# Opening stage of an agent-attention and squared-ReLU kernel: the first batch in 32-column tiles, tables made in place, weight parts decoded in another order

## The chip, the cores and the metric

The kernel runs on one core of a Trainium2 chip. The metric is the device time of one execution in microseconds (us); of several runs the median counts.

Five engines work side by side, each in the order of its own instructions: TensorE (PE, matmuls; its weight loads are listed as PEld), VectorE (DVE), ScalarE (ACT), GpSimd (POOL) and SyncE (SP, which issues the transfers). They wait for each other by semaphores.

## The reference

Four batches of 12,480 queries, keys and values with 128 channels go through an attention by way of 49 agents; each token then goes through a feed-forward layer with 2,048 hidden units.

```python
def sm(a, b):
    s = scale * (a @ b.transpose(0, 2, 1))
    s = s - s.max(-1, keepdims=True)
    e = np.exp(s)
    return e / (e.sum(-1, keepdims=True) + 1e-09)
a2k = sm(agents, k)
agent_v = a2k @ v
q2a = sm(q, agents)
x = (q2a @ agent_v).reshape(B * S, D)     # 49920 x 128
h = np.maximum(x @ w_in, 0.0)             # 128 x 2048
return (h * h @ w_out).astype(np.float32) # 2048 x 128
```

Both weights arrive as 64-bit numbers, which the kernel must turn into 32-bit ones itself.

## The kernel before, in words

**The main loop.** `agent_v @ w_in` is computed once for each batch: a table of 49 rows and 2,048 columns. The hidden layer of a token is then its 49 softmax weights times this table. The table is kept as a rounded part and a remainder (`aw_hi`, `aw_ex`), so that two products on TensorE give nearly 32-bit accuracy: `first(k)` issues for two steps of k together 4 matmuls with `aw_hi` and 4 small ones with `aw_ex`. `hidden(k)` makes r = ReLU (ACT), r times h (DVE; for odd k in place in PSUM), the rounded square `g_hi` (ACT) and its remainder `g_lo` (DVE for odd k, POOL for even k). `second(k)` multiplies these by the second weight, which is also kept as a rounded part and a remainder (`wo_hi`, `wo_lo`), 6 matmuls for each k, LAG = 4 steps later. There are 832 steps of k, 16 for each group of 960 queries (8 for each half), taken in 416 pairs. The queries' softmax of the next group (`queries`) and the attention of the next batch (`background`: `scores`, `maxima`, `values`, `whole_sums`, `tables`) are laid between them in small steps, spread over 0.88 of a batch.

**The opening.** Nothing of the main loop can run before the table of batch 0 exists. While the flag `alone` is set, every instruction goes through `queued`, so each engine's order is the order of the code. The stages are:

- `WARM` dummy matmuls, then the scores of 13 blocks of keys (12 of 8 x 128 keys, one of 192): in each, one matmul of 128 keys against the agents of two batches at once (98 columns, of which 49 are used). DVE keeps a running maximum (`mx`), ACT copies the scores out of PSUM. Between blocks 3 and 10, six of the eight parts of `w_in` are decoded.
- `decoded`: one ACT instruction (absolute value) and five DVE instructions for each part of 256 columns. A part of `w_in` ends in one POOL addition (`make_w_in`), a part of `w_out` in one ACT cast and two POOL operations (`make_w_out`).
- `maxima`: over all keys, through a transpose and two small matmuls; the result is `mb`.
- `whole_exps` (DVE subtraction, ACT exponential), `whole_values` (one matmul for each 128 keys, with the exponentials of two such groups side by side, 98 columns), and `add_weights` (POOL adds up the exponentials for the sums). The other ten weight parts are decoded in between; the last two of `w_out` come after the tables.
- `whole_sums` and `tables`: the four chunks of the table, ACT rounding each into `aw_hi`, DVE writing the remainder into `aw_lo`, and five transfers for each chunk that carry the remainder to other partitions (rows 98 to 127 of `aw_hi`, and four places of `aw_ex`).

Keys and values share a ring of 11 buffers (`ahead`), the raw weight parts a ring of 8 (`raw`), PSUM three double banks (`ps_h`, tiles `h`), one bank for the background (`ps_a`, tiles `psa`) and one for the output (`ps_o`). Line 59 (`queued`) is the line that the profile shows for all that is issued in written order.

Of the kernel before, what the change touches and what calls it, by code (L numbers as in the profile page):

```python
# [29 lines left out]
WARM = 16  # L30
PRE = 11
RAW = 8
# [5 lines left out]
def agent_attention_relu2(ctx: ExitStack, tc: tile.TileContext, qT, kT, v, agT, w_in, w_out, outT):  # L38
# [12 lines left out]
    NQ = P // 32  # L51
    scale = 1.0 / math.sqrt(C)
# [29 lines left out]
    qp = ctx.enter_context(tc.tile_pool(name="qp", bufs=2))  # L82
    ps_h = ctx.enter_context(tc.tile_pool(name="ps_h", bufs=3, space=PSUM))
# [6 lines left out]
    nc.gpsimd.memset(ones, 1.0)  # L90
    ident = const.tile([P, P], F32, name="ident")
# [8 lines left out]
    def asked_for(dec, src):  # L100
        raw = dec.tile([P, WCH, 2], U32, name="raw", bufs=RAW)
# [4 lines left out]
    def ask_w_in(dec, n):  # L106
        return asked_for(dec, w_in.bitcast(U32)[:, 2 * n * WCH : 2 * (n + 1) * WCH])

    def ask_w_out(dec, n):
        c = slice(n * WCH // C, (n + 1) * WCH // C)  # L110
        return asked_for(dec, w_out.bitcast(U32).rearrange("(c p) d -> p c d", p=P)[:, c, :])

    def decoded(dec, raw):
        low, high = raw[:, :, 0], raw[:, :, 1]

        t = dec.tile([P, WCH], U32, name="t")
        act.activation(t.bitcast(F32), high.bitcast(F32), AF.Abs)
# [14 lines left out]
    def make_w_in(dec, n, raw):  # L132
        t, rest = decoded(dec, raw)
        pool.tensor_add(win[:, n * WCH : (n + 1) * WCH], t, rest)

    def make_w_out(dec, n, raw):
        c = slice(n * WCH // C, (n + 1) * WCH // C)
        t, rest = decoded(dec, raw)
# [3 lines left out]
        pool.tensor_add(lo, t, rest)  # L142

# [29 lines left out]
    def scores(b, i, kt):  # L173
        st = state.setdefault(b, {"s": []})
        _, rows, nt = blocks[i]
        if alone[0]:
            h = ps_h.tile([P, 2, 512], F32, name="h")[:rows, :, :].rearrange("p h (t x) -> p h t x", x=P)
            n = nt // 2
            for t in range(nt):
                out = h[:, t // n, t % n, : 2 * NA]  # L180
                keys = kt[:, t * rows : (t + 1) * rows]
                pe.matmul(out, keys, ag[:, :2, :].rearrange("c b a -> c (b a)"), start=True, stop=True)
            sv = h[:, :, :n, :NA]
        else:
            sv = bank()[:rows, : nt * NA].rearrange("p (t a) -> p t a", a=NA)
            for t in range(nt):
                tiled(sv[:, t, :], kt[:, t * rows : (t + 1) * rows], ag[:, b, :])
# [6 lines left out]
        if alone[0]:  # L194
            s, mx = (x.rearrange("p (h t) a -> p h t a", h=2) for x in (s, mx))
# [44 lines left out]
    def whole_values(b, i, vt):  # L240
        st = state[b]
        _, rows, nt = blocks[i]
        e = st["s"][i][:rows, :nt, :]
        if i == 0:
            st["pv"] = ps_h.tile([P, 2, 512], F32, name="h")
        for t in range(nt):
            pair = e[:, t - t % 2 : t - t % 2 + 2, :].rearrange("p t a -> p (t a)")
            pe.matmul(
                st["pv"][:C, t % 2, : 2 * NA], vt[:rows, t, :], pair,
                start=(i == 0 and t < 2), stop=(i == NK - 1 and t >= nt - 2),  # L250
            )

    def add_weights(b, i):
        st = state[b]
        _, rows, nt = blocks[i]
        if i > 0:
            es = st["mx"][:rows, :nt, :]
            pool.tensor_add(es, es if i > 1 else st["s"][0], st["s"][i][:rows, :nt, :])

    def whole_sums(b):  # L260
        st = state[b]
        e1 = small.tile([P, 2, NA], F32, name="e1")
        dve.reduce_sum(e1[:, 0, :], st["mx"].rearrange("p t a -> p a t"), axis=AX.X)
        dve.tensor_copy(e1[:, 1, :], e1[:, 0, :])
        yield
        av = st["avT"] = small.tile([C, K2], F32, name="avT")
        if "pv" in st:
            act.copy(av[:, :NA], st["pv"][:C, 0, :NA])
            dve.tensor_add(av[:, :NA], av[:, :NA], st["pv"][:C, 1, NA : 2 * NA])
        else:  # L270
            dve.tensor_copy(av[:, :NA], st["av"])
        dve.tensor_copy(av[:, NA:], av[:, :NA])
        pz = bank()
        pe.matmul(pz[:K2, :1], e1.rearrange("p h a -> p (h a)"), ones[:, :1], start=True, stop=True)
        rl = st["rl"] = small.tile([K2, 1], F32, name="rl")
        dve.tensor_scalar_add(rl, pz[:K2, :1], 1e-9)
        dve.reciprocal(rl, rl)
# [21 lines left out]
    def tables(b):  # L299
# [3 lines left out]
        ex = st["lo"] = aw.tile([P, NCH // NQ, P], F32R, name="aw_ex")  # L303
        for n in range(FF // 512):
            yield
            cs = slice(n * 512, (n + 1) * 512)
            pw = bank()
            pe.matmul(pw[:K2, :], av, win[:, cs], start=True, stop=True)
# [7 lines left out]
            yield  # L316
# [7 lines left out]
    def queries(g):  # L324
# [10 lines left out]
        dve.reduce_max(m, sv, axis=AX.X)  # L335
        e = qp.tile([TP, NT, NA], F32, name="e", bufs=1)
# [97 lines left out]
    def background(b):  # L434
# [15 lines left out]
        yield from whole_sums(b)  # L450
        yield from tables(b)

    STEPS = NK * 2 + 5 + NK * 4 + 1 + 3 * (FF // 512)
# [13 lines left out]
    NW = FF // WCH  # L467
# [5 lines left out]
    with tc.tile_pool(name="pre", bufs=PRE) as pre, tc.tile_pool(name="dec", bufs=2) as dec:  # L473
        def warm(n):
            idle = bank()
            for _ in range(n):
                pe.matmul(idle[:, :P], ones, ones, start=True, stop=True)

        raws = {}
        kts, vts = [], []  # L480

        def next_values():
            vts.append(load_values(0, len(vts), pre, "ahead"))

        between = {i: n for n, i in enumerate((3, 4, 6, 7, 9, 10))}
        for i in range(NK):
            kts.append(load_keys(0, i, pre, "ahead"))
            if 1 <= i <= NW:
                raws[i - 1] = ask_w_in(dec, i - 1)
            if i == NK - 3:  # L490
                q0 = queries(0)
                next(q0)
            run(scores(0, i, kts[i]))
            if i in between:
                make_w_in(dec, between[i], raws.pop(between[i]))
        next_values()
        for n in range(6):
            next_values()
            raws[NW + n] = ask_w_out(dec, n)
# [5 lines left out]
        next(top)  # L505
        warm(2)
# [3 lines left out]
        for i in range(2):  # L510
            add_weights(0, i)
        between = {i: n for n, i in enumerate((0, 1, 3, 4, 6, 7, 9, 10))}
        for i in range(NK):
            if i + 3 < NK:
                whole_exps(0, i + 3, dve)
            if i + 2 < NK:
                add_weights(0, i + 2)
            if i == NK - 1:
                ends = whole_sums(0)
                next(ends)  # L520
            whole_values(0, i, vts[i])
            next(q0, None)
            if i in between:
                n = between[i]
                if n < 2:
                    make_w_in(dec, NW - 2 + n, raws.pop(NW - 2 + n))
                    next_values()
                    raws[2 * NW - 2 + n] = ask_w_out(dec, NW - 2 + n)
                else:
                    make_w_out(dec, n - 2, raws.pop(NW + n - 2))  # L530
            if i >= 2 and len(vts) < NK:
                next_values()
        run(q0)
        run(ends)
        ahead = queries(1)
        next(ahead)
        run(tables(0))
        next(ahead)
        next(ahead)
        for n in range(NW - 2, NW):  # L540
            make_w_out(dec, n, raws.pop(NW + n))
    behind = [chain[eng] for eng in (nc.sync, nc.scalar, nc.vector, nc.gpsimd)]

    alone[0] = False
    ffn = ctx.enter_context(tc.tile_pool(name="ffn", bufs=4))
    todo = iter(())
    for k in range(total + LAG):
        if k < total:
            g, c = divmod(k, SLOTS)
            b, i = divmod(g, NB)  # L550
            if i == 0 and c == 0 and b + 1 < B:
                todo = background(b + 1)
                done = 0
            goal = (i * SLOTS + c + 1) * STEPS / (SPREAD * NB * SLOTS)
# [5 lines left out]
            if c >= 2 or g == 0:  # L560
# [46 lines left out]
```

## Time and profile before

| | |
|---|---|
| median of 3 runs | 2005.19 us (2005.07 to 2005.92) |
| the profiled execution: its time, its span | 2006.08 us, 2004.3 us |
| PE, PEld, DVE, ACT, POOL busy in the span | 98%, 74%, 84%, 86%, 59% |
| transfers: share of the 16 DMA engines | 19.9% |
| first `r` of the main loop (ACT) | at 96.97 us |

The busy shares are means over the whole span. In the 40 slices of the profile (50 us each) the first slice and a part of the second and third are the opening; from there on the slices are alike.

### The profile page before, as it was taken

The page shows a single profiled execution, that of the slowest core. Times are in us where ns is not written, and L with a number is a line of the kernel's source. Part 1 is how long each engine was busy: PE and PEld are TensorE (multiplying, and loading weights), DVE is VectorE, ACT ScalarE, POOL GpSimd, SP SyncE. Part 2 cuts the span into 40 slices and gives each one's busy share as a digit, 9 for nine tenths or more (in the row PEclk, how much of TensorE's full clock was granted, in tenths as well). Part 3 has the DMA queues.
Part 4 walks back from the last instruction along what each step waited for, and adds up shares of the span by engine and source line. Part 5 has one row for each costly group of instructions (what it writes and reads, how often), then busy time and mean ns, then how long its engine had stood idle before and what let it go on. Part 6 is the DMA issues. An engine that isn't in the chain of part 4 may idle for free. (4 is left out here: it accounts for less than half of the span.)

```text
span 2004.3 us, 44157 instructions
## 1 busy us (share of the span) xinstructions
PE 1966.5 (98%) x17240; PEld 1486.0 (74%) x17240; DVE 1677.2 (84%) x1852; ACT 1729.8 (86%) x2019; POOL 1191.0 (59%) x1054
## 2 busy tenths in 40 slices
PE   8699999999999999999999999999999999999999
PEld 7477777777777777777777777777777777777777
DVE  5678878888888888888888888888888888898887
ACT  2388888889988888889988898898999999999997
POOL 1545676655555666656555576665565656565555
PEclk8799999999999999999999999999999999999999
DMA  8242222111122221211122211211111111111100
GB/s 313 72 137 75 88 73 77 59 61 47 50 89 83 70 77 59 66 66 50 49 67 89 67 56 59 86 56 38 54 38 43 38 46 37 37 47 38 33 24 20
DMA packets 55991, 132.14 MB, mean 66 GB/s; under 512 B 6712, under 2 KB 35336, under 8 KB 55784
## 3 DMA queue, kind: packets, MB, share of 16 engines
q1 hardware_dynamic: 55784, 129.33, 19.9%
q8 instruction: 136, 2.23, 0.5%
q14 instruction: 71, 0.58, 0.1%
HBM read 80.97 MB, written 25.56 MB: 53 GB/s over the span
## 5 line engine op out<-in xcount | busy, mean ns | idle before, releaser
L405 POOL TENSOR_TENSOR g_lo<-gg,g_hi 128x480 fp32r<-128x480 f32 x832 | 999.9, 1223 | 706.1 <-DVE gg L59 458.8
L59 ACT ACTIVATE r<-h 128x960 f32<-128x960 f32 x832 | 801.8, 964 | 127.2 <-PE h L59 117.3
L59 ACT ACTIVATE g_hi<-r 128x960 fp32r<-128x960 f32 x832 | 837.6, 1007 | 35.5 <-issue 0.4
L59 DVE TENSOR_TENSOR h<-r,h 128x960 f32<-128x960 f32 x416 | 482.0, 1159 | 158.7 <-ACT r L59 153.5
L59 PE MATMUL o<-g_hi,wo_hi 128*128 128x480 f32 x1664 | 542.7, 407 | 0.6 <-DVE z L344 0.6
L59 DVE TENSOR_TENSOR gg<-r,h 128x960 f32<-128x960 f32 x416 | 477.6, 1148 | 44.2 <-ACT r L59 41.1
L59 DVE TENSOR_TENSOR g_lo<-h,g_hi 128x960 fp32r<-128x960 f32 x416 | 480.7, 1155 | 36.2 <-ACT g_hi L59 2.2
L59 PE MATMUL o<-g_hi,wo_lo 128*128 128x480 f32 x1664 | 499.3, 381 | 0.0
L59 PE MATMUL o<-g_lo,wo_hi 128*128 128x480 f32 x1664 | 497.8, 380 | 0.0
L59 PE MATMUL h<-w,aw_hi 128*128 128x480 f32 x1664 | 475.4, 397 | 14.4 <-DVE gg L59 12.3
L59 PEld LDWEIGHTS o<-g_hi,wo_hi 128*128 128x128 f32 x1664 | 280.8, 188 | 119.9 <-issue 65.2
L59 PEld LDWEIGHTS o<-g_lo,wo_hi 128*128 128x128 f32 x1664 | 312.6, 188 | 51.3
L59 PEld LDWEIGHTS o<-g_hi,wo_lo 128*128 128x128 f32 x1664 | 312.7, 188 | 51.1
L59 PEld LDWEIGHTS h<-w,aw_hi 128*128 128x128 f32 x1664 | 292.1, 189 | 73.2 <-DVE gg L59 21.0
L59 PE MATMUL h<-x,aw_ex 19*128 19x480 f32 x1664 | 204.0, 480 | 0.0
L59 PEld LDWEIGHTS h<-x,aw_ex 19*128 19x128 f32 x1664 | 80.0, 182 | 139.5 <-issue 139.2
L59 DVE COPY ob<-o 128x480 f32<-128x480 f32 x104 | 68.2, 656 | 41.5 <-PE o L59 41.4
L354 PEld LDWEIGHTS psa<-identr,pp 120*98 120x98 f32 x408 | 51.7, 165 | 8.9
L359 ACT CAST w<-psa 98x480 fp32r<-98x480 f32 x102 | 55.5, 544 | 2.4 <-PE h L59 0.5
L226 POOL TENSOR_TENSOR pp<-e,pp 120x392 fp32r<-120x392 f32 x51 | 49.3, 967 | 11.4 <-ACT pp L224 11.4
L345 POOL TENSOR_TENSOR e<-e,z 120x392 f32<-120x392 f32 x51 | 43.1, 845 | 16.1 <-ACT d L286 8.6
L171 PEld LDWEIGHTS psa<-ag,qt 128*32 128x32 f32 (+1 forms) x3200 | 37.9, 108 | 16.8 <-issue 15.8
(110 smaller groups left out, 845.9 us busy)
## 6 DMA issues: line engine op xcount, KB each, us to landing
qt<-in_qT SPq DMA_DIRECT2D x52, 480.0 KB
out_T<-ob SPq DMA_DIRECT2D x104, 240.0 KB
kt<-in_kT SPq DMA_DIRECT2D x36, 512.0 KB
vt<-in_v SPq DMA_DIRECT2D x36, 512.0 KB
x<-w SPq DMA_DIRECT2D x416, 35.6 KB
ahead<-in_kT SPq DMA_DIRECT2D x12, 512.0 KB
ahead<-in_v SPq DMA_DIRECT2D x12, 512.0 KB
w<-w SPq DMA_DIRECT2D x104, 56.2 KB
```

Source lines behind the costliest of these rows:

```text
L59: ins = issue(*args, **kw)
L171: pe.matmul(out[at:up, :], stationary[:, at:up], moving, start=start, stop=stop)
L226: eng.tensor_sub(out[:, :, n : n + w], x, out[:, :, :w].bitcast(F32))
L345: pool.tensor_mul(e, e, z.broadcast_to([TP, NT, NA]))
L354: pe.matmul(pt[:K2, t * TP : (t + 1) * TP], pp[:, j * (NT // 2) + t, :], identr, start=True, stop=True)
L359: act.copy(w[:K2, :], pt[:K2, :G])
L405: nc.gpsimd.tensor_sub(lo[:, n, :], gg[:, n, :], hi[:, n, :].bitcast(F32))
```

## The change

- The scores of batch 0 are computed like the background's: four matmuls with 32 stationary columns each (`tiled`), for one batch only (49 columns).
- `whole_values` uses the same tiles. A fifth matmul for each 128 keys, with ones as its 32 stationary columns, sums the exponentials into columns 49 to 97 of the same bank; the 128 keys take the four column places in turn. `add_weights` (POOL) is gone, and `shares` (1/32) takes out the 32 equal rows in `ready`, which replaces `whole_sums`.
- `tables` makes each remainder in the partitions where it is needed: the stationary `avT` is widened to 128 columns by repetition, an extra chunk (n = -1, 16 matmuls in 32-column tiles) gives all of `aw_ex`, and the 20 transfers are gone. For each of the four chunks, ACT now makes a rounded copy of rows 96 to 127 (`near`), DVE writes the remainder of these rows into `aw_hi`, and ACT then writes rows 0 to 97. This holds for all four batches.
- The loads come in another order (two parts of `w_in` ahead of the first keys, values and `w_out` parts behind the keys without a step of work between). ACT's part of a decoding is issued one part ahead (`begun`). All of `w_in` is decoded during the scores, three parts of `w_out` during the values, and the last five (`LATE`) in the first five pairs of the main loop.
- The background and the queries of group 1 start at k = 4 (`BEGIN`) and not at k = 0. There are `warm` matmuls between the blocks of values.

```diff
-WARM = 16
+WARM = 14
-RAW = 8
+RAW = 10
+LATE = 5
+BEGIN = 4
...
+    def begun(dec, raw):
+        t = dec.tile([P, WCH], U32, name="t")
+        act.activation(t.bitcast(F32), raw[:, :, 1].bitcast(F32), AF.Abs)
+        return dec, raw, t
...
     def scores(b, i, kt):
-        if alone[0]:
...
-                pe.matmul(out, keys, ag[:, :2, :].rearrange("c b a -> c (b a)"), start=True, stop=True)
...
+        sv = bank()[:rows, : nt * NA].rearrange("p (t a) -> p t a", a=NA)
+        for t in range(nt):
+            tiled(sv[:, t, :], kt[:, t * rows : (t + 1) * rows], ag[:, b, :])
...
     def whole_values(b, i, vt):
-            pair = e[:, t - t % 2 : t - t % 2 + 2, :].rearrange("p t a -> p (t a)")
-            pe.matmul(
-                st["pv"][:C, t % 2, : 2 * NA], vt[:rows, t, :], pair,
...
+            if not last:
+                tiled(pv[:C, :NA], vt[:rows, t, :], e[:, t, :], start=first, stop=False)
+            q = t % NQ * CT
+            pe.matmul(pv[q : q + CT, NA:K2], ones[:rows, :CT], e[:, t, :], start=False, stop=False)
...
-    def add_weights(b, i):
...
+    def ready(b):
+        if "pv" in st:
+            wide(act.copy, av, st["pv"][:C, :NA])
+            wide(dve.tensor_copy, ew, st["pv"][:, NA:K2])
...
+        pe.matmul(pz[:, :1], ew, share, start=True, stop=True)
+        for t in range(NQ):
+            pe.matmul(pz[t * CT : (t + 1) * CT, 2:3], ew[:, SP : SP + CT], share, start=True, stop=True)
...
     def tables(b):
-        for n in range(FF // 512):
+        for n in range(-1, FF // 512):
...
-            act.activation(hi[:K2, cs], pw[:K2, :], AF.Copy, scale=rl)
-            lo = aw.tile([NA, 512], F32R, name="aw_lo", bufs=3)
...
+            act.activation(near[rows, :], pw[rows, :], AF.Copy, scale=rl[rows, r : r + 1])
             dve.scalar_tensor_tensor(
-                out=lo, in0=pw[:NA, :], scalar=rl[:NA, :], in1=hi[:NA, cs].bitcast(F32),
+                out=out[rows, :], in0=pw[rows, :], scalar=rl[rows, r : r + 1], in1=near[rows, :].bitcast(F32),
                 op0=ALU.mult, op1=ALU.subtract,
             )
-            sync.dma_start(hi[K2:, cs].bitcast(F32), lo[:SP, :].bitcast(F32))
-            for t in range(NQ):
-                sync.dma_start(ex[t * 32 : t * 32 + NL, n, :].bitcast(F32), lo[SP:, t * P : (t + 1) * P].bitcast(F32))
+            if n >= 0:
+                act.activation(hi[:K2, cs], pw[:K2, :], AF.Copy, scale=rl[:K2, :1])
...
+        between = {i: n + NW for n, i in enumerate((2, 4, 6))}
...
+            whole_values(0, i, vts[i])
+            warm(1)
...
         if k % 2 == 0:
             hs = first(k) if k < total else ()
+            if held:
+                alone[0] = True
+                part = decoded(*begun(late, held[0]))
             if hs:
                 hidden(k, hs[0])
+            if held:
+                kept(2 * NW - len(held), *part)
+                held.pop(0)
+                alone[0] = False
```

**DVE during the scores.** Before, DVE's order opens with four blocks' maxima (`mx`) and then decodes one part at a time:

```order
L59 COPY mx<-h 128x392
L59 TENSOR_TENSOR mx<-mx,h 128x392 x3
L59 TENSOR_SCALAR t<-t 128x256 x2
L59 SCALAR_TENSOR_TENSOR t<-raw,t 128x256
L59 TENSOR_SCALAR rest<-t 128x256
L59 SCALAR_TENSOR_TENSOR rest<-raw,rest 128x256
L59 TENSOR_TENSOR mx<-mx,h 128x392
```

Now two parts are decoded first; this is the second of them and what follows:

```order
L62 TENSOR_SCALAR t<-t 128x256 x2
L62 SCALAR_TENSOR_TENSOR t<-raw,t 128x256
L62 TENSOR_SCALAR rest<-t 128x256
L62 SCALAR_TENSOR_TENSOR rest<-raw,rest 128x256
L62 COPY mx<-h 128x392
L62 TENSOR_TENSOR mx<-mx,h 128x392
```

Eight decodings stand among the 13 maxima where six stood.

**PE from the values to the main loop.** Before (`s` are the exponentials, `ahead` the values, `pp` the queries' weights on their way to a transpose):

```order
L59 MATMUL h<-dg,ones 128x49
L59 MATMUL h<-s,ahead 128x98 x48
L59 MATMUL h<-identr,pp 98x120 x4
L59 MATMUL h<-s,ahead 128x98 x16
L59 MATMUL h<-identr,pp 98x120 x4
L59 MATMUL h<-s,ahead 128x98 x34
L59 MATMUL h<-ones,e_719 98x1
L59 MATMUL h<-win,avT 98x512 x4
```

Now, from the last 128 keys on:

```order
L62 MATMUL h<-s,ones 32x49 x2
L62 MATMUL h<-s,ahead 32x49 x4
L62 MATMUL psa<-ones 32x128 x4
L62 MATMUL h<-shares,ew 128x1
L62 MATMUL h<-shares,ew 32x1 x4
L62 MATMUL psa<-ones 32x128 x8
L62 MATMUL psa<-win,avT 32x128 x16
L62 MATMUL h<-win,avT 128x512 x4
L62 MATMUL h<-w_1257,aw_hi 128x480 x4
```

Each 128 keys take five small matmuls where half a matmul of two batches' width stood, dummy matmuls stand behind each block, and the scores of group 1 (32 matmuls on `qt`) no longer stand between the tables and the first pair.

**ACT at the tables.** Before, with `t<-raw` and `wo_hi<-t` as the two ACT instructions of a `w_out` part:

```order
L59 COPY avT<-h 128x49
L59 ACTIVATE aw_hi<-h,rl 98x512 x4
L59 ACTIVATE t<-raw 128x256
L59 CAST wo_hi<-t 128x256
L59 ACTIVATE t<-raw 128x256
L59 CAST wo_hi<-t 128x256
L339 ACTIVATE e<-e 120x392
L59 ACTIVATE r<-h 128x960
```

Now, from the last chunk on:

```order
L62 ACTIVATE near<-h,rl 32x512
L62 ACTIVATE aw_hi<-h,rl 98x512
L62 ACTIVATE t<-raw 128x256
L62 ACTIVATE r<-h 128x960
L62 ACTIVATE g_hi<-r 128x960
L62 CAST wo_hi<-t 128x256
L62 ACTIVATE r<-h 128x960
```

The two decodings that stood ahead of the first `r` are now spread, with three more, over the first five pairs, one in each; on DVE a pair begins with the decoding and then has its `gg`, `h` and `g_lo`.

More of the change, by code (lines that the diff above doesn't have):

```diff
@@ L100, in asked_for @@
     def asked_for(dec, src):
-        raw = dec.tile([P, WCH, 2], U32, name="raw", bufs=RAW)
+        raw = dec.tile([P, WCH, 2], U32, name="raw", bufs=LATE if dec is late else RAW)
         flat = raw.rearrange("p n w -> p (n w)")
@@ L130, in decoded, with kept @@
         return t.bitcast(F32), rest
[L132 to L138, printed above, removed]
+    def kept(n, t, rest):
+        if n < NW:
+            pool.tensor_add(win[:, n * WCH : (n + 1) * WCH], t, rest)
+            return
+        c = slice((n - NW) * WCH // C, (n - NW + 1) * WCH // C)
         hi, lo = (x[:, c, :].rearrange("p c d -> p (c d)") for x in (wo_hi, wo_lo))
@@ L142, in make_w_out, with made @@
         pool.tensor_add(lo, t, rest)
+    def made(n, part):
+        kept(n, *decoded(*part))
     def bank():
@@ L244, in whole_values @@
         if i == 0:
-            st["pv"] = ps_h.tile([P, 2, 512], F32, name="h")
+            st["pv"] = bank()
+        pv = st["pv"]
         for t in range(nt):
-            pair = e[:, t - t % 2 : t - t % 2 + 2, :].rearrange("p t a -> p (t a)")
-            pe.matmul(
-                st["pv"][:C, t % 2, : 2 * NA], vt[:rows, t, :], pair,
-                start=(i == 0 and t < 2), stop=(i == NK - 1 and t >= nt - 2),
-            )
-    def add_weights(b, i):
-        st = state[b]
[L255 to L264, printed above, removed]
-        yield
[L266 to L276, printed above, removed]
+            first, last = i == 0 and t == 0, i == NK - 1 and t == nt - 1
@@ L471, in agent_attention_relu2, with warm, asks, begins @@
         pe.matmul(idle[:, 0, :P], ones, ones, start=True, stop=True)
[L473 to L479, printed above, removed]
-        kts, vts = [], []
-        def next_values():
-            vts.append(load_values(0, len(vts), pre, "ahead"))
-        between = {i: n for n, i in enumerate((3, 4, 6, 7, 9, 10))}
+    def warm(n):
+        idle = ps_a.tile([P, 512], F32, name="psa")
+        for _ in range(n):
+            tiled(idle[:, :P], ones, ones)
+    with tc.tile_pool(name="pre", bufs=PRE) as pre, tc.tile_pool(name="dec", bufs=3) as dec:
+        raws, parts0 = {}, {}
+        kts, vts = [], []
+        def asks(n):
+            raws[n] = ask(dec, n)
+        def begins(n):
+            parts0[n] = begun(dec, raws.pop(n))
+        def makes(n):
+            if n + 1 in raws and n + 1 != NW:
+                begins(n + 1)
+            made(n, parts0.pop(n))
+        asks(0)
+        asks(1)
         for i in range(NK):
             kts.append(load_keys(0, i, pre, "ahead"))
-            if 1 <= i <= NW:
-                raws[i - 1] = ask_w_in(dec, i - 1)
-            if i == NK - 3:
+            if 1 <= i < NW - 1:
+                asks(i + 1)
+            if i == NW - 1:
                 q0 = queries(0)
                 next(q0)
+        for i in range(NK):
+            vts.append(load_values(0, i, pre, "ahead"))
+            if i % 2 == 0 and i // 2 < NW - LATE:
+                asks(NW + i // 2)
+        begins(0)
+        makes(0)
+        makes(1)
+        between = {i: n + 2 for n, i in enumerate((1, 2, 4, 5, 6, 8))}
+        for i in range(NK):
             run(scores(0, i, kts[i]))
+            if i == NK - 3:
+                next(q0)
             if i in between:
[L495 to L499, printed above, removed]
+                makes(between[i])
         top = maxima(0)
@@ L505, in agent_attention_relu2 @@
         next(top)
+        next(q0)
         warm(2)
@@ L509, in agent_attention_relu2 @@
             whole_exps(0, i, dve)
-        for i in range(2):
-            add_weights(0, i)
-        between = {i: n for n, i in enumerate((0, 1, 3, 4, 6, 7, 9, 10))}
+        next(q0)
+        between = {i: n + NW for n, i in enumerate((2, 4, 6))}
         for i in range(NK):
@@ L515, in agent_attention_relu2 @@
                 whole_exps(0, i + 3, dve)
[L516 to L520, printed above, removed]
-            whole_values(0, i, vts[i])
-            next(q0, None)
-            if i in between:
[L524 to L532, printed above, removed]
+            whole_values(0, i, vts[i])
+            warm(1)
+            if i < 3 or i > 7:
+                next(q0, None)
+            if i == 0:
+                begins(NW)
+            if i == NK - 4:
+                held = [ask(late, 2 * NW - LATE + n) for n in range(LATE)]
+                ahead = queries(1)
+                next(ahead)
+            if i in between:
+                makes(between[i])
         run(q0)
-        run(ends)
-        ahead = queries(1)
-        next(ahead)
+        run(ready(0))
+        warm(2)
         run(tables(0))
[L538 to L542, printed above, removed]
+    behind, done = [], 0
     alone[0] = False
     ffn = ctx.enter_context(tc.tile_pool(name="ffn", bufs=4))
-    todo = iter(())
     for k in range(total + LAG):
+        if k == BEGIN:
+            behind = [chain[eng] for eng in (nc.tensor, nc.sync, nc.scalar, nc.vector, nc.gpsimd)]
         if k < total:
```

84 lines of the change are left out of this document (55 added, 29 removed).

## The prediction, before any run of the changed kernel

> **What bounds the kernel now.** I read the page first, for the share of each engine in the slices of the span:
>
> ```profile
> span 2004.3 us, 44157 instructions
> PE   8699999999999999999999999999999999999999
> PEclk8799999999999999999999999999999999999999
> ```
>
> PE is full from the third slice (50 us each) to the end; only the opening has gaps, and a lower granted clock. Then the busy times by stretches, which I cut where the stages change: scores, maxima, values, tables, first pairs, the rest.
>
> ```profile
> core 0: us, PE busy (x) PEld busy (x) DVE busy (x) ACT busy (x) POOL busy (x), PEclk, DMA share, GB/s
> 0.00:36.50 36.50, 30.09 (x292) 29.29 (x292) 16.86 (x43) 9.25 (x20) 5.18 (x13) 1.00 0.98 364
> 36.50:41.50 5.00, 2.49 (x12) 2.13 (x12) 2.81 (x7) 0.89 (x4) 0.00 (x0) 0.63 0.84 313
> 41.50:74.80 33.30, 29.13 (x204) 28.66 (x204) 25.00 (x49) 11.64 (x27) 22.53 (x23) 0.80 0.32 103
> 74.80:97.00 22.20, 9.77 (x85) 4.20 (x84) 15.10 (x33) 5.93 (x14) 6.71 (x9) 0.74 0.10 29
> 97.00:110.30 13.30, 10.64 (x90) 6.93 (x90) 9.61 (x10) 12.16 (x14) 8.05 (x8) 0.53 0.63 236
> 110.30:2004.30 1894.00, 1884.40 (x16560) 1414.79 (x16559) 1607.80 (x1714) 1689.98 (x1944) 1148.50 (x1002) 1.00 0.18 58
> ```
>
> After 110.3 us PE works 1884.4 of 1894.0 us at full clock. The loop can get shorter only by less PE work, and the change adds a little. So the question is how much earlier the loop reaches its full rate. In the opening no engine bounds alone: the transfers are at 0.98 during the scores, PE at 29.1 of 33.3 us during the values at a mean clock of 0.80, and in the 22.2 us of the tables nobody is busy. For that I read the timeline, PE first:
>
> ```profile
> 33.48 0.90 PE L59 MATMUL h<-ag,qt 128*32 128x49 f32 x64 [1.53 <-ACT s L59]
> 37.49 0.28 PE L59 MATMUL h<-ident,m 128*49 128x128 f32 x1 [3.11 <-DVE m L59]
> 41.48 14.07 PE L59 MATMUL h<-s,ahead 128*128 128x98 f32 x96 [1.52 <-ACT s L59]
> 72.35 2.47 PE L59 MATMUL h<-s,ahead 128*128 128x98 f32 x20 [0.44 <-ACT s L59]
> 80.16 0.46 PE L59 MATMUL h<-ones,e 128*98 128x1 f32 x2 [5.34 <-DVE avT L59]
> 99.18 1.17 PE L59 MATMUL h<-w,aw_hi 128*128 128x480 f32 x2 [7.38 <-DVE gg L59]
> 101.44 1.53 PE L171 MATMUL psa<-ag,kt 128*32 128x49 f32 x64 [0.39 <-DMA kt<-in_kT]
> ```
>
> Each 32-bit matmul leaves two records. The values end at 74.8 us; then PE waits 5.34 us, because DVE still decodes, and later 7.38 us, because the first `r` of the loop comes late. DVE and ACT, the rows that I price with:
>
> ```profile
> 16.32 0.62 DVE L59 TENSOR_SCALAR t<-t 128x256 f32<-128x256 f32 x2 [0.89 <-ACT t L59]
> 18.11 0.55 DVE L59 TENSOR_TENSOR mx<-mx,h 128x392 f32<-128x392 f32 x1
> 36.52 0.81 DVE L59 TENSOR_REDUCE m<-mx 128x49 f32<-128x392 f32 x1
> 40.24 2.00 DVE L59 TENSOR_TENSOR s<-s,mb 128x392 f32<-128x392 f32 x4
> 57.77 1.61 DVE L59 TENSOR_SCALAR t<-t 128x256 f32<-128x256 f32 x2 [1.05 <-ACT t L59]
> 80.86 0.16 DVE L59 RECIPROCAL rl<-rl 98x1 f32<-98x1 f32 x1
> 82.53 0.69 ACT L59 ACTIVATE aw_hi<-h,rl 98x512 fp32r<-98x512 f32 x1 [4.19 <-PE h L59]
> 83.25 0.74 DVE L59 SCALAR_TENSOR_TENSOR aw_lo<-h,rl,aw_hi 49x512 fp32r<-49x512 f32 x1 [2.23 <-ACT aw_hi L59]
> 89.20 0.74 DVE L59 SCALAR_TENSOR_TENSOR aw_lo<-h,rl,aw_hi 49x512 fp32r<-49x512 f32 x1 [1.89 <-DMA aw_ex<-aw_lo]
> 96.97 0.97 ACT L59 ACTIVATE r<-h 128x960 f32<-128x960 f32 x1 [1.33 <-POOL wo_lo L59]
> 121.42 1.16 DVE L59 TENSOR_TENSOR g_lo<-h,g_hi 128x960 fp32r<-128x960 f32 x1
> ```
>
> The first `r` waits for POOL's end of the last decoded part, not for a transfer. The row at 121.42 is the last DVE work of the fifth pair (k = 8, 9); it ends at 122.6, and I use it as the mark against which the new opening is measured. Last, groups by line and shape, for prices:
>
> ```profile
> L59 DVE TENSOR_TENSOR h<-r,h 128x960 f32<-128x960 f32 x416 | 482.0, 1159 | 158.7 <-ACT r L59 153.5
> L59 DVE TENSOR_TENSOR gg<-r,h 128x960 f32<-128x960 f32 x416 | 477.6, 1148 | 44.2 <-ACT r L59 41.1
> L308 PE MATMUL psa<-win,avT 128*98 128x512 f32 x24 | 12.2, 592 | 0.0
> L59 PE MATMUL h<-ones 128*128 128x128 f32 x40 | 8.5, 404 | 1.0 <-POOL ones L90 1.0
> L59 ACT ACTIVATE t<-raw 128x256 f32<-128x256 f32 x16 | 6.9, 429 | 0.0
> L59 ACT CAST wo_hi<-t 128x256 fp32r<-128x256 f32 x8 | 3.2, 404 | 16.9 <-DVE t L59 16.9
> L59 ACT COPY avT<-h 128x49 f32<-128x49 f32 x1 | 0.2, 197 | 0.0
> L342 DVE TENSOR_REDUCE z<-e 120x8 f32<-120x392 f32 x51 | 28.2, 554 | 0.1
> L343 DVE TENSOR_SCALAR z<-z 120x8 f32<-120x8 f32 x51 | 34.4, 675 | 1.0
> ```
>
> **The change, step by step.** Times are those of the profiled span.
>
> *1. Scores.* A block of 8 x 128 keys costs PE 0.90 us in tiles (row at 33.48, also 64 records), so PE is out of the way. Two limits are left. DVE has eight decodings of 1.79 us (16.32 to 18.11) and 13 maxima of 0.55 us, 21.5 us from the landing of the first part, which I put at 5 to 6 us: 27. The transfers have keys 6.39 MB, `w_in` 2.10, queries 0.49 and agents 0.10, together 9.08 MB; at the 364 GB/s of the first stretch that is 24.9 us, and landing, one block's scores and the last maxima lie behind. I take 29.0 us for the first instruction of the maxima where 36.52 stands now (27.3 to 30.5). The ACT instruction issued one part ahead takes the wait of 0.89 us out of each decoding; without that DVE would be the limit at 34.
>
> *2. Maxima.* From 36.52 to the first matmul on values at 41.48 are 4.96 us; the same links stay: 34.0. The new warm matmuls stand in the same place, as many columns as before.
>
> *3. Values.* Five matmuls for each 128 keys make 80 records a block: 0.90 x 80/64 = 1.13 us, and the four dummy tiles 0.21 to 0.42 us (8.5 us / 20 matmuls is 0.42 on a slow clock), I take 0.27. That is 1.40 us a block, 12.25 blocks: 17.2, so the values end at Z = 51.2. The values have landed by then: 16.3 MB at 364 GB/s are 45 us. Bound below: DVE has 13 subtractions of 0.5, three decodings and the queries' sums, 13.6 us from 32.5 on, so Z = 48.2 if PE keeps up. Bound above: the half clock. The row at 101.44 shows the same 64 records at 1.53 us, which gives 2.35 us a block and Z = 62.8. POOL's additions are gone, and with them what doubled DVE's tensor operations (1.61 us at 57.77 against 0.62 at 16.32).
>
> [...] The wait of 3.11 us ahead of 37.49 was followed by a clock of 0.50:
>
> ```profile
> 32.00:37.00 5.00, 0.90 (x64) 1.00 1.05 383
> 38.00:48.00 10.00, 8.48 (x40) 0.50 0.34 120
> ```
>
> In the new order I count gaps of 1.9 us ahead of the maxima and 2.3 ahead of the values; the wait of 1.53 at 33.48 did not lower it. So I take the full clock. [...]
>
> [...]
>
> *4. From Z to the first `r`.* Six small copies of 0.2 us, DVE's behind ACT's since they read the same bank: 1.25 us. Sums, dummies, the extra chunk (16 tiles, 0.85 by columns from step 1) and the first chunk on PE (12.2 / 12 = 1.02): 4.05. The reciprocal, 0.86 us from 80.16 to its end at 81.02, fits beside them. Then each chunk is a chain: ACT 0.69, DVE 0.74, ACT 0.69, since rows 96 and 97 are written by both; 2.1 us, four of them 8.4. The first `r` follows one short ACT instruction later: Z + 12.7, 63.9 instead of 96.97. The transfers removed are worth at most their 1.89 us ahead of 89.20 here; they were nearly hidden. What goes is the decoding ahead of `rl` and ahead of `r`.
>
> *5. The five late parts.* DVE then has for each of five pairs 3 x 1.155 = 3.46 us and a decoding of 1.79, which grows beside a busy POOL (by 1.0 at 57.77; I take 0.7): 5.95 each, 29.8; two maxima and one query group's five operations at 0.2 to 0.7 add 3.7. From Z + 12.8 the fifth pair ends at Z + 46.3 = 97.5, where 122.6 stands: 25.1 us won. PE, at 4.57 us a pair (1894.0 over some 414 pairs), waits for DVE here; ACT has 0.83 more a pair (0.43 and 0.40, the groups of `t<-raw` and `wo_hi`) and stays below DVE.
>
> *6. The loop behind.* The scores of group 1 move into it: 0.9 us. Three more tables cost PE 16 tiles and four sums each, 1.0: 3.0. The bank `psa` is held for 2.1 us a chunk instead of 1.4; I take 1 for that. Together 5 (0 to 10).
>
> Sum: 2004.3 - 25.1 + 5 = 1984.2, 20.1 below. The profiled execution took 2006.08; the median is 2005.19, so 1985.
>
> **The rivals.**
> - *The values run slowly.* At the half clock, 11.6 more: 1997; or the fifth matmul always waits for its own column place, so that each 128 keys take two rounds instead of 1.25: 1.80 + 0.27 us a block, 8.2 more: 1993. For it: no row shows five in a round, and the three waits over 3 us shown above (3.11, 5.34, 7.38) were all followed by stretches below full clock. Against it: the shorter gaps.
> - *The opening is limited by its feed and no more.* Z = 48.2, decodings at 1.79 beside POOL (3.5 less), the loop's extras hidden: 1985 - 3 - 3.5 - 4 = 1974.
> - *Slower: the later tables stop PE.* In the loop, PE is in order and `psa` is one bank, also used by scores and queries. If PE stands for the whole 2.1 us in all 15 chunks, 31.5 us are lost, less the 1 counted: 2015. It decides from 1.5 us a chunk on. Against it: the row of `psa<-win,avT` shows 0.0 us idle ahead of 24 records, at 1.4 us a chunk.
> - *Little comes of it.* Half clock, and five late pairs of 8 us because ACT and POOL are late as well, 10 more: 2007 at the worst, 2002 to 2007 with half the rest.
>
> **How the numbers follow.** The forecast (1975 to 1991) gets 0.62, slow values 0.18, the feed limit 0.10, stopped tables 0.05, little 0.05. The range 1972 to 1999 takes in the bounds of steps 3, 5 and 6 and most of the second and third case. 0.2% (4 us) is about what a measurement tells from no change: faster 0.91, same 0.03, slower 0.06.
>
> **What would show it.** The maxima near 29 us; values at about 1.4 us a block with PEclk 1.00 up to about 51; chunks of 2.1 us on ACT; the first `r` near 64; five pairs of about 6 us with DVE nearly full; the fifth pair's `g_lo` near 97; then pairs as before. I am wrong if PE shows 0.5 during the values, if a block takes 1.8 us or more, or if PE in the loop waits for ACT ahead of `psa<-win`.

## The result and the profile after

The changed kernel takes 2026.81 us (median; 2024.09 to 2028.22), the kernel before 2005.56 us beside it (2005.07 to 2005.99). The ratio is 1.0104 with a 95% interval of 1.0087 to 1.0122: slower by 21 us, where 20 us less was forecast. The profiled execution took 2026.45 us and its span is 2024.7 us. Its page, with PE's busy time and PE's clock in the 40 slices:

```profile
span 2024.7 us, 47364 instructions
PE   5689999999999999999999999999999999999999
PEclk7889999999999999999999999999999999999999
```

From the fourth slice on PE's digits are those of before. The loss is in the first 150 us, and PE, which has more instructions there, is *less* busy: 5, 6 and 8 tenths in the first three slices, where 8, 6 and 9 stood. The stages, in us of the span, by the marks of the prediction (the last column is the last experiment, below):

| | before | forecast | changed | last experiment |
|---|---|---|---|---|
| first instruction of the maxima | 36.52 | 29.0 | 42.71 | 34.11 |
| first matmul on values | 41.48 | 34.0 | 47.75 | 38.54 |
| last matmul on values (Z) | 74.8 | 51.2 | 77.9 | 64.2 |
| first `r` | 96.97 | 63.9 | 95.84 | 77.06 |
| end of the fifth pair's `g_lo` | 122.6 | 97.5 | 127.4 | 109.5 |
| end of the span | 2004.3 | 1984.2 | 2024.7 | 1999.6 |

The marks of the changed kernel, from the timeline of DVE and ACT:

```profile
42.71 0.81 DVE L62 TENSOR_REDUCE m<-mx 128x49 f32<-128x392 f32 x1
95.84 0.96 ACT L62 ACTIVATE r<-h 128x960 f32<-128x960 f32 x1
126.21 1.16 DVE L62 TENSOR_TENSOR g_lo<-h,g_hi 128x960 fp32r<-128x960 f32 x1
```

What PE waits for in the scores, the values, the tables and behind the mark, from its timeline. The bracket at the end of a row is the idle time ahead of it and what ended it:

```profile
13.82 3.39 PE L62 MATMUL h<-ag,ahead 128*32 128x49 f32 x128 [2.09 <-ACT s L62]
17.52 0.20 PE L62 MATMUL h<-ag,ahead 128*32 128x49 f32 x1 [0.30 <-DMA ahead<-in_kT]
19.90 2.20 PE L62 MATMUL h<-ag,ahead 128*32 128x49 f32 x127 [2.18 <-issue]
25.88 2.84 PE L62 MATMUL h<-ag,ahead 128*32 128x49 f32 x127 [3.78 <-issue]
31.73 2.85 PE L62 MATMUL h<-ag,ahead 128*32 128x49 f32 x127 [3.02 <-issue]
47.75 0.39 PE L62 MATMUL h<-s,ahead 128*32 128x49 f32 x8 [1.47 <-ACT s L62]
56.64 0.23 PE L62 MATMUL h<-s,ahead 128*32 128x49 f32 x1 [2.12 <-issue]
60.33 0.23 PE L62 MATMUL h<-s,ones 128*32 128x49 f32 x1 [1.78 <-issue]
63.90 0.20 PE L62 MATMUL h<-s,ahead 128*32 128x49 f32 x1 [1.81 <-issue]
85.37 3.66 PE L62 MATMUL h<-win,avT 128*128 128x512 f32 x4 [2.28 <-ACT aw_hi L62]
91.82 1.57 PE L62 MATMUL h<-win,avT 128*128 128x512 f32 x2 [2.79 <-ACT aw_hi L62]
141.62 0.48 PE L62 MATMUL h<-x,aw_ex 19*128 19x480 f32 x1 [0.72 <-DMA x<-w]
143.22 0.49 PE L62 MATMUL h<-x,aw_ex 19*128 19x480 f32 x1 [1.13 <-DMA x<-w]
```

Three things are new. "issue" is time in which PE waits for nothing that the profile shows. These gaps come at fixed places in the instruction stream, not in the data: after every 127 or 128 records in the scores, inside a block whose keys are there (one record of a block at 17.52, then 2.18 us of nothing), and every 3.6 to 4.0 us in the values up to 67.85. In the tables PE waits for ACT ahead of the second and the fourth chunk. And behind the mark the loop waits for group 1's `x`. The sum over the opening, from the view of waits:

```profile
PE h L62 <- issue: 22.1, 11, 3.8
PE h L62 <- ACT aw_hi L62: 5.1, 2, 2.8
```

22.1 us in 11 gaps; the kernel before has no gap named issue in its first 110 us. With each record goes one weight load (18,908 of each in the changed kernel), so 128 records are 256 instructions. The queue that the page names instruction shows the same from the other side (packets, MB, share), before and after:

```profile
q8 instruction: 136, 2.23, 0.5%
```

```profile
q8 instruction: 149, 2.44, 0.5%
```

13 packets more with 0.21 MB, 16 KB each. PE has 1,668 more matmul records (18,908 against 17,240) and as many more weight loads: 3,336 instructions, and 13 packets of 256 are 3,328. This is the theory for the experiments: **a sustained stream of tiled matmuls runs no faster than PE's instructions are brought in, one packet of 256 at a time.** The rival of the prediction was the half clock.

### The profile page after: what moved, and what is told of

It is laid out like the page before. It is cut to its first block, busy times and chain, and to the rows that moved or that the text cites. A ratio compares the mean times of both kernels' runs of the same rounds, so it can differ in the third digit from the quotient of the medians.

```text
span 2024.7 us, 47364 instructions
## 1 busy us (share of the span) xinstructions
PE 1966.2 (97%) x18908; PEld 1475.2 (73%) x18908; DVE 1678.5 (83%) x1861; ACT 1740.5 (86%) x2041; POOL 1177.2 (58%) x1043
## 5 line engine op out<-in xcount | busy, mean ns | idle before, releaser
L62 PE MATMUL h<-w,aw_hi 128*128 128x480 f32 x1664 | 475.9, 397 | 10.9 <-DVE gg L62 10.6
L179 PEld LDWEIGHTS psa<-ag,qt 128*32 128x32 f32 x3264 | 38.6, 108 | 17.3 <-issue 16.0
```

The lines of the kernel that those rows point to most:

```text
L62: ins = issue(*args, **kw)
L179: pe.matmul(out[at:up, :], stationary[:, at:up], moving, start=start, stop=stop)
```

## The experiments

The changed kernel is the starting point of all but the first. Ratios are to the kernel before, measured beside each.

**1. The supply alone.** A kernel with nothing of the reference in it: 640 tiled matmuls of the scores' form with one and the same operand, nothing to wait for, then 128 whole ones; both again beside a stream of loads.

```python
small(640)   # four column places in turn, 32 stationary columns, 49 moving
large(128)   # 128 stationary columns, 98 moving
...          # 70 loads of 0.5 MB
small(640)
large(128)
```

> This kernel computes nothing of the reference; it measures TensorE alone: 640 tiled matmuls (32x49, 1280 records) and 128 whole ones (128x98) without transfers, then both again under a stream of 512 KB loads. Theory (instruction supply: the gaps named issue come once in 128 records, i.e. 256 instructions with their weight loads): without transfers a gap after each 128 tiled records and some 3.6 us per 128 (28 ns a record, 36 us for the stretch), under loads some 5.9 us per 128 (46 ns a record, 59 us); the whole matmuls run without gaps at 0.225 us each in both. Rival (half clock, or waits for a column place): no gaps at multiples of 128, 14 ns a record at full clock (18 us) or 24 ns at half (31 us), alike with and without loads.

PE's timeline:

```profile
13.19 1.59 PE L62 MATMUL tiles<-ones 128*32 128x49 f32 x128 [1.45 <-issue]
16.64 1.59 PE L62 MATMUL tiles<-ones 128*32 128x49 f32 x128 [1.86 <-issue]
23.82 2.84 PE L62 MATMUL tiles<-ones 128*32 128x49 f32 x128 [1.22 <-issue]
27.28 1.87 PE L62 MATMUL tiles<-ones 128*32 128x49 f32 x128 [0.62 <-issue]
34.18 1.59 PE L62 MATMUL tiles<-ones 128*32 128x49 f32 x128 [1.86 <-issue]
42.27 28.83 PE L62 MATMUL whole<-ones 128*128 128x98 f32 x256
99.57 2.84 PE L62 MATMUL tiles<-ones 128*32 128x49 f32 x128 [3.36 <-issue]
105.76 2.29 PE L62 MATMUL tiles<-ones 128*32 128x49 f32 x128 [3.36 <-issue]
```

The gap stands after each 128 records, one step per 3.45 us with idle transfer queues (13.19 to 16.64) and one per 5.9 to 6.2 us (99.57 to 105.76) under loads at 408 GB/s. The data can't cause it, there is none to wait for. The clock doesn't set the pace either: the packet at 23.82 took 2.84 us instead of 1.59 (the clock was 0.61 from 20 to 25 us and 0.71 from 25 to 30, where it was 1.00 from 10 to 20), and the next one still began 3.46 us behind it; only the gap got shorter. Whole matmuls take 28.83 us for 256 records, so 14.4 us for each 128, and have no gap. The instruction queue moved 24 packets with 0.39 MB for this kernel's 6,276 PE instructions, 24.5 times 256. The supply is shown, at 3.45 us for 256 instructions. It sizes the changed kernel too: the values are 12.25 blocks of 88 records (80 and four dummy tiles), with their loads 2,156 instructions, 8.4 packets, at 3.45 us 29.1 us; they took 30.2.

**2. Scores without tiles, 49 columns.** One whole matmul for each 128 keys and one batch, a fourth of the instructions.

```diff
-            tiled(sv[:, t, :], kt[:, t * rows : (t + 1) * rows], ag[:, b, :])
+            pe.matmul(sv[:, t, :], keys, ag[:, b, :], start=True, stop=True)   # while alone
```

> The changed kernel with one part undone: the first batch's scores by one whole matmul for each 128 keys (49 columns) instead of four tiles. Theory (instruction supply): a quarter of the instructions, so the gaps of 13 us in the scores go; 12.25 blocks of 8 x 0.225 us from 7.5 on, the maxima begin at 30 to 33 us instead of 42.7, and the time falls by 9 to 12 us. Rival (the scores are held by transfers or by DVE, and the gaps are only where PE waits it out): the maxima still begin after 40 us and the time moves by less than 2 us.

2030.13 us, ratio 1.0124 (1.0109 to 1.0139): not faster. The gaps named issue are gone from the scores, but the maxima begin at 46.28. Windows of this run (all engines: PE, PEld, DVE, ACT, POOL, then clock, share of the transfers, GB/s):

```profile
8.00:12.00 4.00, 4.00 (x38) 4.00 (x38) 2.65 (x7) 1.25 (x4) 0.73 (x1) 1.00 1.03 407
16.00:20.00 4.00, 4.00 (x21) 4.00 (x20) 0.76 (x2) 0.48 (x1) 0.65 (x1) 0.50 1.03 417
```

and the same stretch of the kernel before, which has 98 columns in each matmul:

```profile
16.00:20.00 4.00, 4.00 (x38) 4.00 (x38) 2.62 (x8) 1.11 (x3) 0.73 (x1) 1.00 1.04 401
```

PE is busy for the whole of both stretches. With 98 columns it keeps the full clock; with 49, at the same rate of matmuls at first (38 records in 4 us), the clock falls to 0.50 and the rate with it. So the cure removed one limit and met another. Neither the theory (maxima at 30 to 33) nor its rival (gaps that only fill a wait) is what happened.

**3. Each chunk of the tables in a tile of its own.** The four chunks share two tiles, and PE waits for ACT's read of chunk 0 ahead of chunk 1.

```diff
-                pair = ps_h.tile([P, 2, 512], F32, name="h") if n % 2 == 0 else pair
-                pw = pair[:, n % 2, :]
+                pw = bank()
```

> The changed kernel with one change: in the opening each chunk of the table gets a PSUM tile of its own, where two chunks shared one. Theory (PE's waits of 2.28 and 2.79 us ahead of chunks 1 and 3 come from the shared tile: the second chunk's matmul waits for ACT's last read of the first): both waits go, the first r comes 4 to 5 us earlier and the time falls by 4 to 5 us. Rival (the chain near, remainder, aw_hi on ACT and DVE sets the pace, and the waits only fill it): less than 1.5 us.

2024.95 us, ratio 1.0097 (1.008 to 1.0114). The first chunk on ACT, in the changed kernel and in this one:

```profile
83.12 0.68 ACT L62 ACTIVATE near<-h,rl 32x512 fp32r<-32x512 f32 x1 [0.35 <-PE h L62]
```

```profile
84.41 0.68 ACT L62 ACTIVATE near<-h,rl 32x512 fp32r<-32x512 f32 x1 [0.66 <-PE h L62]
```

From there to the first `r` ACT needs 9.1 us (84.41 to 93.48) where it needed 12.7 (83.12 to 95.84), and its chunks follow each other at 2.2 us. The first chunk itself came 1.3 us later, so the first `r` comes only 2.4 us earlier. PE's waits for ACT shrink from 5.1 to 3.5 us and don't go: what is left is the chain of the rival. In the time the 1.9 us can't be told from the spread of the changed kernel's own runs.

**4. The background from the start of the loop.**

```diff
-BEGIN = 4
+BEGIN = 0
```

> The changed kernel with the background and the queries of group 1 starting at k = 0, as before the change. Theory (the late start makes the transfers of x for group 1 late: four waits of together 3.6 us at 141 to 146 us, and half clock behind them): the waits go, the time falls by 5 to 7 us. Rival (the same work then falls into the first pairs, which DVE and ACT bound, and is paid there): within 2 us.

2021.31 us, ratio 1.0079 (1.0063 to 1.0094), 5.5 us less. The waits for `x` are gone, and the loop behind the mark takes 1889.1 us instead of 1897.3. The later start cost more than the 0.9 us that the moved scores were worth to the prediction.

**5. Scores as before,** one matmul of 98 columns for two batches; the rest of the change stays.

```diff
-            tiled(sv[:, t, :], kt[:, t * rows : (t + 1) * rows], ag[:, b, :])
+                pe.matmul(out, keys, ag[:, :2, :].rearrange("c b a -> c (b a)"), start=True, stop=True)
```

> The changed kernel with the first batch's scores as they were before the change: one whole matmul for each 128 keys on 98 columns. [...]

The question was whether the clock of 0.50 in experiment 2 goes with its 49 columns or with the new order of loads and decodings. At full clock, with 0.225 us a matmul (14.43 us for the 128 records from 7.55 on in the kernel before), the maxima were estimated at 31 to 34 us and the time at 2016 to 2018; at half clock the maxima after 45 us, and 2028 to 2032.

2017.89 us, ratio 1.0065 (1.005 to 1.008), 8.9 us less. PE in the scores (busy, clock, share of the transfers, GB/s), and the first instruction of the maxima:

```profile
10.00:20.00 10.00, 9.62 (x83) 1.00 1.03 414
```

```profile
32.56 0.81 DVE L62 TENSOR_REDUCE m<-mx 128x49 f32<-128x392 f32 x1
```

32.56 instead of 42.71, at full clock. The loads in their new order and the decodings one part ahead are worth 4 us against the 36.52 of before, with the old matmuls.

**6. Both stages without tiles.** Scores and values by matmuls of 98 columns with POOL's sums, no dummies between the values, and edits 3 and 4.

> The changed kernel without column tiles in the opening: scores and values of the first batch by whole matmuls on 98 columns and the sums on POOL, as before the change, no dummies between the values; the background starts at k = 0 and each chunk of the table has its own PSUM tile. What stays of the change: the order of loads and decodings, five late parts, tables made in place. Theory (the tiles' instruction supply and the clock are what made it slower, the rest of the change is a gain): maxima at 32, values from 37 to 61, first r near 77, the mark of the fifth pair near 109, time about 2000 (1995 to 2006). Rival (the late parts and tables in place cost as much as they bring): 2010 to 2016, above the kernel before.

2010.75 us, ratio 1.0028 (1.0018 to 1.0039). Better by 16 us than the change, but not the 2000 expected: the number lies in the rival's range. The trace shows another reason than the rival's. The opening was now short enough to meet a transfer. PE, ACT and SP in the timeline:

```profile
36.93 19.33 PE L62 MATMUL h<-s,ahead 128*128 128x98 f32 x144 [1.53 <-ACT s L62]
82.28 1.53 PE L179 MATMUL psa<-ag,kt 128*32 128x49 f32 x64 [12.56 <-DMA kt<-in_kT]
86.52 0.97 ACT L62 ACTIVATE r<-h 128x960 f32<-128x960 f32 x1 [11.01 <-issue]
```

```profile
72.42 0.89 SPq L164 DMA_DIRECT2D kt<-in_kT  x2
```

SP asks for the background's first keys at 72.42, behind the weight parts, the queries and the pieces of group 0, and PE stands for 12.56 us on them, with all of the main loop behind it.

**7. No dummies between the values** (the `warm(1)` taken out, tiles kept).

> The changed kernel without the dummy matmuls between the blocks of values (52 matmuls, 208 instructions). Theory (instruction supply bounds the values): 0.8 of a refill of 3.45 us less, so the values take 26 to 27 us instead of 29.2 and the time falls by 2 to 3.5 us. Rival (the dummies hold the clock up): half clock in the values and 3 to 8 us more.

2026.21 us, ratio 1.0103 (1.0088 to 1.0118): no difference. 104 records fewer, with their loads 208 instructions, should save 0.8 of a packet, 2.8 us; the values took 29.2 us, 1.0 less than the 30.2 of the changed kernel. The gaps still stand after each 127 or 128 records, 3.8 to 4.2 us apart. The mean clock was lower than with the dummies (0.67 to 0.89 in stretches of 10 us, against 0.83 to 1.00), but experiment 1 showed the same pace, 3.45 us, at a clock of 1.00 and at 0.61 to 0.71. So theory and rival are both missed, and why the packets come more slowly here is not shown.

**8. Values as before,** scores in tiles, no dummies.

```diff
-                tiled(pv[:C, :NA], vt[:rows, t, :], e[:, t, :], start=first, stop=False)
+            pe.matmul(st["pv"][:C, t % 2, : 2 * NA], vt[:rows, t, :], pair, ...)   # and add_weights on POOL
```

> The changed kernel with the values and their sums as before the change (one whole matmul for each 128 keys on 98 columns, sums on POOL), no dummies; scores still in tiles. Theory (instruction supply): no gaps named issue in the values, 22 to 26 us for them instead of 29.2, and 3 to 7 us less in all. Rival (DVE and POOL again hold each other up, with the sums' additions): the values take 30 to 33 us, and the time is the same or 2 to 4 us more.

2023.21 us, ratio 1.0091 (1.0074 to 1.0108). Each 128 keys take one whole matmul again, as in the kernel before. The values take 26 us (47.80 to 73.8) without a gap named issue, as the theory said; the rival's 30 to 33 us did not come. The first `r` comes at 89.64 and the mark at 122.5. The time gained is 3.6 us, at the low end of the theory's 3 to 7, though single runs of the two kernels overlap; the late `x` is still there (four waits, 3.6 us).

**9 to 11. What the untiled opening is held by.** Edits of experiment 6 with other starts of the background, and with fewer late parts:

```diff
-BEGIN = 0            # 6
+BEGIN = 4            # 9
+BEGIN = 2            # 10, 11
-LATE = 5
+LATE = 3             # 11: five parts of w_out among the values
```

> The first batch of both stages by whole matmuls of 98 columns with POOL's sums, each table chunk in a tile of its own, no matmuls between the values, the background at k = 4 as in the changed kernel. Theory (kt was late in the run with BEGIN = 0 only because the opening had become shorter than SP's queue): no wait for kt ahead of the first r, which comes at 75 to 78 us (62.8 + 13 to 15); fifth pair's g_lo 31 to 33 later, near 108; then 3.6 us of waits for x<-w; loop behind the mark 1889 + 5.5 = 1894.6; span near 2003, time 2001 to 2006. Rival (the tables or the late parts hold the first r, not kt): r stays near 86, time 2012 or more.

2008.91 us, ratio 1.0017 (1.0008 to 1.0025). The first `r` comes at 77.93, as the theory said, so neither the tables nor the late parts held it in experiment 6. The mark at 110.8 is 2.8 us later than expected, and the time is 3 us above its range: PE waits for the late `x` again (3.4 us), and the loop behind the mark takes 1897.2.

> The same with the background at k = 2. Theory: kt has landed by then (needed near 83 us, landed near 82 in the run with BEGIN = 0), and x<-w comes a pair earlier, so both waits go or nearly: first r 75 to 78, mark near 109, loop behind 1889 to 1891, time 1998 to 2003, below the kernel before. Rival: kt is still late by some microseconds, or x<-w is, 2003 to 2008.

2006.72 us, ratio 1.0003 (0.9994 to 1.0012). The waits for `x` are gone and the first `r` comes at 75.43, but `kt` is still late, now behind the first pair, as the rival said; the mark is at 113.0. (The profiled execution is the fastest of eleven, 2003.57 us.) PE's waits between 75 and 130:

```profile
PE psa L179 <- DMA kt<-in_kT: 7.2, 1, 7.2
PE h L62 <- DVE gg L62: 3.5, 2, 1.9
```

> As the run before, with LATE = 3: five parts of w_out decoded during the values and three in the first pairs. Theory (DVE bounds the first pairs, 1.8 us and more for each late part): the values get 1 to 3 us longer, since DVE was busy 22.2 of 25.9 us there, the first pairs 3 to 5 us shorter, time 0 to 3 us lower. Rival (DVE is full in the values, each part costs there what it saves later, or more): no change or 1 to 3 us more.

2003.61 us, ratio 0.9991 (0.9982 to 1.0), 3.1 us below the run before. The way from the first `r` to the mark takes 30.0 us, where the run before took 37.6 with 7.2 us of waiting for `kt` in them. But the values and the tables' start get later (first `r` at 81.21), and by then `kt` has landed. So the gain can be the wait that went as well as the two parts: theory and rival are not told apart by this one.

**12. The transfer of the first keys asked for earlier,** ahead of the late weight parts; else as 10.

```diff
+                soon = load_keys(1, 0, kv, "kt")
                 held = [ask(late, 2 * NW - LATE + n) for n in range(LATE)]
```

> The run with the background at k = 2, and the transfer of its first keys (kt) asked for ahead of the five late raw parts (near 62.9 us) instead of behind them, the queries and the pieces of group 0 (72.1 us). Theory (PE's 7.2 us ahead of the first kt scores are the landing of that transfer): the wait goes, the fifth pair's g_lo comes 31 to 33 us behind the first r at 75 to 76, so near 107 to 109 where it was 113; loop behind it 1889; span 1996 to 1998, and the median 3 to 6 us below the run with the background at k = 2, so 2000 to 2004, below the kernel before. Rival (the late raw parts land later instead, or the first pairs are bound by DVE all the same and the wait for kt was partly under it): 0 to 2 us less.

2001.87 us against 2005.15 of the kernel before, ratio 0.9984 (0.9975 to 0.9993): the fastest version, 3.3 us below before, 25 below the change and 4.9 below experiment 10, as the theory said, with its marks 0.5 to 1.6 us later than the theory had them. PE's wait for `kt` is gone. Its timeline (PE, ACT, DVE):

```profile
38.54 18.85 PE L62 MATMUL h<-s,ahead 128*128 128x98 f32 x144 [1.52 <-ACT s L62]
64.72 0.53 PE L62 MATMUL h<-ones,ew 128*128 128x1 f32 x10 [0.57 <-DVE avT L62]
77.06 0.96 ACT L62 ACTIVATE r<-h 128x960 f32<-128x960 f32 x1
108.36 1.16 DVE L62 TENSOR_TENSOR g_lo<-h,g_hi 128x960 fp32r<-128x960 f32 x1 [0.19 <-ACT g_hi L62]
```

The first `r` comes 19.9 us earlier than before the change, the fifth pair's end only 13.1 (DVE holds the pairs, with the late parts in them: of PE's waits between 75 and 130, 5.2 us are for its `gg`), and of that the loop behind gives back 8.4 (1890.1 against 1881.7). The span is 4.7 us shorter.

## Why the prediction was wrong, step by step

The forecast span was 1984.2, the measured one is 2024.7: 40.5 us, which the steps share as 13.7 + 0 + 13.0 + 5.2 - 2.1 + 10.6 (rounded).

*1. Scores: 29.0 forecast, 42.71 measured (+13.7). The step that failed.* "A block costs PE 0.90 us in tiles" was read from 64 records that stood alone in the loop's entry. That is the price of a burst shorter than a packet. In the stream of the scores the next 128 records began 5.7 to 6 us later beside loads at 304 to 413 GB/s (19.90, 25.88, 31.73, 37.41), about 2.9 us a block. DVE and the transfers, which the step weighed against each other, were not the limit; DVE stood waiting for PE:

```profile
32.01 0.56 DVE L62 TENSOR_TENSOR mx<-mx,h 128x392 f32<-128x392 f32 x1 [3.96 <-PE h L62]
```

The clock fell in this stage too, which the step did not expect. All engines from 20 to 30 us:

```profile
20.00:30.00 10.00, 4.93 (x254) 4.55 (x255) 5.16 (x13) 2.12 (x5) 1.86 (x3) 0.53 1.03 413
```

At 0.53 PE was still idle for half of the stretch, so the packets set the pace; without the gaps the clock would have set it (0.50 in experiment 2, with PE busy for 4.00 of 4 us). Experiment 5 gives the size: with 98 columns the maxima begin at 32.56, which is still above the step's range (27.3 to 30.5), so 10.2 of the 13.7 are the tiles and 3.6 the step's own optimism on DVE and the feed.

*2. Maxima: 4.96 forecast, 5.04 measured.* Right.

*3. Values: 17.2 forecast, 30.2 measured (+13.0). Failed for the same reason.* The bound above (28.8, the half clock) was nearly the size, and the rival "the values run slowly" had the chance of 0.18; but its cause is not what happened: the mean clock was 0.88, and at 58 to 68 us it was 1.00 while PE was busy for 4.38 of 10 us:

```profile
58.00:68.00 10.00, 4.38 (x303) 4.00 (x292) 5.88 (x11) 2.53 (x5) 3.33 (x4) 1.00 0.02 3
```

A price of 14 ns for a record (0.90 us for 64), used in both steps, was right for the burst and beside the point for the stage. The step took the clock from the lengths of the gaps; in experiment 2 it fell to 0.50 without one (PE busy for 4.00 of 4 us from 8 to 12 and from 16 to 20). No rival named the supply, so the range had no room for two stages failing together.

*4. From Z to the first `r`: 12.7 forecast, 17.9 measured (+5.2).* The chain of 2.1 us a chunk was right: with own tiles the chunks follow at 2.2 us, and from Z to `r` experiment 10 measures 12.9 (62.5 to 75.43) and experiment 12 as much. What the step missed is in the code that it read: chunks 0 and 1 share a tile, as do 2 and 3, and PE waits with the second half until ACT and DVE have read the first (2.28 and 2.79 us). Experiment 3 puts 3.6 us on it; about 1 us more is the first chunk, which came 5.2 us behind Z where some 4 were counted.

*5. Five late pairs: 33.6 us forecast from the first `r` to the mark, 31.5 measured.* Right in mechanism and size. DVE is late, PE waits for `gg` (4.5 us up to 110 us).

*6. The loop behind: +5 forecast (0 to 10), +15.6 measured against the 1881.7 of before.* With BEGIN = 0 the excess is 7.4 us (experiments 4 and 6), more than the 5 taken: the extra tiles of the three later tables take 5.1 us of PE, where 2.6 (3 x 0.85) were counted. No run shows the 0.85: the extra chunk of the opening took 1.08 us, those of the loop 1.7 each. From the groups by line of experiment 6:

```profile
L338 PE MATMUL psa<-win,avT 128*32 128x128 f32 x96 | 5.1, 279 | 0.0
```

The rest is the group-1 queries that start four steps later: `x` then arrives behind its first use, four waits with 3.6 us together, and a fall of the clock (0.68 from 140 to 150 us). The step listed what was moved into the loop and not what waits for it there. Experiment 4 undoes it: 8.2 us in this stretch, 5.5 in the time, since the scores of group 1 stand ahead of the first pair again and the first `r` came 2.6 us later in it.

The rival on the other side, later tables that stop PE, did not occur; "little comes of it" reached 2007 and went by the clock as well. The signs given for being wrong did show (a block at 1.8 us or more: 2.5 us), but they were put down to the wrong cause. What the prediction hoped for from the loads' order and the tables is real: 33 us were to be won at the first `r`, and without the tiles 20 to 21.5 are (experiments 12 and 10). Of that 3.3 us reach the end.

## What to carry to other kernels

Price a sustained stream of small matmuls by its instructions, weight loads included, and not by the records of a short burst. Here PE ran through 256 instructions of the tiles in 1.59 us and got them once in 3.45 us (5.9 to 6.2 beside loads of 408 GB/s, experiment 1), so their supply was the limit, and four small matmuls in place of a large one lost 10.2 us in the scores (42.71 against 32.56, experiment 5). When an opening gets shorter, go through every transfer that the next stage needs and ask when the queue issues it; here `x` and `kt` took back 5.5 and 4.9 us in their turn (experiments 4 and 12). The gaps that the profile put down to issue, one for each 256 instructions and also where there was no data to wait for (experiment 1), were such a supply; count the instruction packets of both kernels before looking at clocks.

## What the runs showed of the hardware

- PE's instructions came in packets of 256 (16 KB): 13 more with 0.21 MB for the 3,336 more instructions of the change, and 24 with 0.39 MB for the 6,276 of experiment 1. With nothing else to do PE ran through one of tiled 32 x 49 matmuls in 1.59 us and waited 1.86 us for the next: one per 3.45 us, and one per 5.9 to 6.2 us while loads moved 408 GB/s.
- PE that was busy without a break didn't keep the full clock for that alone: 98 moving columns per whole matmul kept 1.00 (16 to 20 us in the kernel before, and 10 to 20 us in the new order of experiment 5), 49 at the same number of matmuls were at 1.00 from 8 to 12 us and at 0.50 from 16 to 20 (experiment 2), PE busy for 4.00 of 4 us in these rows and for 9.62 of 10 in that of experiment 5. What separates the row of the kernel before from the first of experiment 2 is how many columns stream per us: 38 records in 4 us are 19 matmuls, so 466 columns per us against 233.
- What stays open: why the clock in the values was lower (0.67 to 0.89 against 0.83 to 1.00) and the packets slower (3.8 to 4.2 us apart) without the dummies, though PE's gaps were of the same kind (experiment 7), and what the clock follows; a sweep over the number of columns wasn't run.
